# Sparse attention and two MLPs: how and when the weights are converted, and the order of the instructions

## The chip, the cores and the metric

The kernel runs on one core of one Trainium2 chip. The metric is the device time in microseconds (us); the kernel before took 1215.54 us, the median of three runs (1215.2 to 1216.38). TensorE is called PE here, VectorE DVE, ScalarE ACT, GpSimd POOL; SP is the engine whose queue issues all of the kernel's DMAs.

## The reference

```python
# q, k, v: 4 batches, 8 heads, 576 positions, head width 64, float32
scores = q @ k.T / sqrt(64)
keep only scores >= (row maximum - tau), softmax over the kept ones
x = (attn @ v) with heads side by side          # 2304 tokens x 512
h = x @ w_in                                    # 512 -> 2048
g = max(h, 0) + alpha * min(h, 0)
x = g @ w_out                                   # 2048 -> 512
h = x @ w2_in
g = where(h > 0, h, exp(min(h, 0)) - 1)
out = g @ w2_out
```

The weights of both MLPs arrive as 64-bit floats, 32 MiB in all.

## The kernel before

**Attention.** A unit is a batch and a pair of heads; 16 units of 9 jobs each make 144 jobs, a job being 128 query rows (or the 64 left over of both heads). A table of due times (`AT`, line 353) gives each stage of a job its place, and everything of the attention stage is issued through the `Pinned` wrappers (line 78), which keep the written order on each engine. In the trace such instructions carry line 84.

**The weights.** PE multiplies in fp32r, so each weight is kept as a high and a low part. A piece is the input half (`part` 0) or the output half (`part` 1) of block f of one layer, 128 partitions x 512; there are 2 layers x 16 blocks x 2 = 64 pieces. `conversion` (line 115) takes a piece from the 64-bit words: two ACT operations (lines 126, 127), two DVE operations (129, 130), a DVE and a POOL operation (133, 135), ACT writes the high part (137), DVE the low part (139) and the load of the piece three places on is issued. It is a generator of five steps, and one piece is worked on at a time.

The first 8 blocks of layer 0 (`FIRST`, 16 pieces) are converted beside the attention jobs, one step for every 1.5 jobs (`beside`, line 501). The last 8 blocks are converted in the first chunk of layer 0, where `convert_to` (line 154) runs two pieces to their end ahead of each block's first use. The 32 pieces of layer 1 are converted in the last chunk of layer 0, as blocks come free, and in the first chunk of layer 1. There the engines are the plain ones (not pinned), and a scheduler orders the instructions by priority; the activation's instructions (`tc.high_priority`, line 418) go ahead.

**The MLPs.** Tokens go in chunks of 512: four whole chunks and one of 256 for each layer. For each of 16 blocks f, `hidden` (line 408) runs 12 matmuls into one PSUM bank (line 415), and DVE, ACT and POOL make from it the activation's high and low part (lines 421 to 432); two blocks later (`LAG`) `outer` (line 441) runs 12 matmuls (452 or 455) into four accumulators. After the last block `evacuate` (line 435) moves accumulators 0 and 2 by ACT and 1 and 3 by DVE into `o`, which has two buffers, and a DMA stores each one; the third evacuation so waits for the first one's store. `load_in` (line 390) fetches the next chunk's input in four parts and splits each into high (ACT, 404) and low (DVE, 405). For the very first chunk it runs beside the last attention jobs, through the pinned engines (lines 499 to 505).

**The start.** `load_unit` (line 176) loads each head's k and q in the order k, q, q's tail for each half; `tau` is loaded after the first unit and its values (line 488), and the scale `sc` (line 491) made from it is needed by the first evacuations of q.

Of the kernel before, what the change touches and what calls it, by code (L numbers as in the profile page):

```python
# [20 lines left out]
def sparse_attention_two_mlps(  # L21
# [29 lines left out]
    FIRST = 8  # L51
# [6 lines left out]
    inp = ctx.enter_context(tc.tile_pool(name="inp", bufs=1))  # L58
# [8 lines left out]
    sc = const.tile([P, 1], F32, name="sc")  # L67
    alpha = const.tile([P, KFF], F32, name="alpha")
    x_d = [dram.tile([P, KDM, S], F32, name=f"x{b}") for b in range(B)]
    y_d = [dram.tile([P, KDM, M], F32, name=f"y{c}") for c in range(NCH)]  # L70
# [15 lines left out]
    plain = nc.vector, nc.scalar, nc.gpsimd  # L86
    pe, dve, act, pool = (Pinned(engine) for engine in (nc.tensor, nc.vector, nc.scalar, nc.gpsimd))
    pinned = dve, act, pool
# [26 lines left out]
    def conversion(dve, act, pool):  # L115
        i = converted[0]
        converted[0] += 1
        layer, f, part = pieces[i]
        if part == 0:
            wt[layer, f] = wps[f >= FIRST].tile([P, 2, 2, DM], F32R, tag="w", name="w")  # L120
        hi, lo = wt[layer, f][:, part, 0, :], wt[layer, f][:, part, 1, :]
# [7 lines left out]
        dve.tensor_scalar(out=x, in0=x, scalar1=TOP, scalar2=BOTTOM, op0=ALU.min, op1=ALU.max)  # L129
        dve.tensor_scalar(out=bits, in0=bits, scalar1=5, scalar2=2,  # L130
                                op0=ALU.logical_shift_left, op1=ALU.logical_shift_right)
        yield
        dve.scalar_tensor_tensor(out=bits, in0=upper, scalar=0xC0000000, in1=bits,  # L133
                                       op0=ALU.bitwise_and, op1=ALU.bitwise_or)
        pool.tensor_tensor(out=bits, in0=bits, in1=t, op=ALU.add)  # L135
        yield
        act.activation(out=hi, in_=x, func=AF.Copy)  # L137
        yield
# [3 lines left out]
    started = [None]  # L142


    def convert_step(limit, engines=plain):
        if started[0] is None:
            if converted[0] >= limit:
                return False
            started[0] = conversion(*engines)
        if next(started[0], "end") == "end":  # L150
            started[0] = None
        return True

    def convert_to(layer, f):
        n = 2 * (layer * KFF + f) + 2
        while convert_step(n) and (converted[0] < n or started[0] is not None):
            pass

    def w_in(layer, f, kk, part):
        return wt[layer, f][:, 0, part, kk * P:(kk + 1) * P]  # L160

    def w_out(layer, f, part):
        return wt[layer, f][:, 1, part, :]
# [12 lines left out]
    def load_unit(u):  # L176
# [3 lines left out]
        raws[u] = []  # L180
        for h in range(2):
            kr = raw.tile([KB, HS // KB, P], F32, tag="kr", name="kr", bufs=4)
            qr = raw.tile([P, NKT + 1, P], F32, tag="qr", name="qr", bufs=4)
            for a, cols in halves():
                rows = k[b, 2 * hp + h, a * HS:(a + 1) * HS, :]
                nc.sync.dma_start(out=kr[:, :, cols], in_=rows.rearrange("(t p) d -> p t d", p=KB))
                rows = q[b, 2 * hp + h]
                nc.sync.dma_start(out=qr[:, 0:NKT, cols], in_=rows[0:MAIN, :].rearrange("(t p) d -> p t d", p=P))
                nc.sync.dma_start(out=qr[0:TAIL, NKT, cols], in_=rows[MAIN:S, :])
            raws[u].append((kr, qr))  # L190
# [15 lines left out]
    def prep(u, i):  # L206
# [4 lines left out]
        if i < 2:  # L211
            kr = raws[u][i][0]
            for t in range(HS // KB):
                pe.transpose(ps[:, t * KB:(t + 1) * KB], kr[:, t, :], ident[0:KB, 0:KB])
        if i == 0:
            for h in range(2):
                pe.transpose(ps[:, HS + h * TAIL:HS + (h + 1) * TAIL], raws[u][h][1][0:TAIL, NKT, :],
                             ident[0:TAIL, 0:TAIL])
        if i >= 2:
            qr = raws[u][i - 2][1]  # L220
            for t in range(NKT):
                pe.transpose(ps[:, t * P:(t + 1) * P], qr[:, t, :], ident)
        return ps

    def keep_prep(u, i, ps):
        kt, qt = turned_in[u]
        if i < 2:
            act.activation(out=kt[:, i, :], in_=ps[:, 0:HS], func=AF.Copy)
# [3 lines left out]
        if i >= 2:  # L232
            act.activation(out=qt[:, i - 2, 0:MAIN], in_=ps, func=AF.Copy, scale=sc)
# [123 lines left out]
    def attention(beside):  # L357
# [24 lines left out]
        for i in range(2 * len(jobs) // 3):  # L382
            put(1.5 * i + AT["beside"], beside, 1.5 * i)
# [6 lines left out]
    def load_in(layer, j, dve=nc.vector, act=nc.scalar):  # L390
        n = min(M, NT - j * M)
        hi, lo = (inp.tile([P, KDM, M], F32R, tag="in", name="in", bufs=4) for _ in range(2))
        for kk in range(KDM):
            r = inp.tile([P, M], F32, tag="r", name="r", bufs=3)
            at = 0
            while layer == 0 and at < n:
# [148 lines left out]
```

## Time and profile before

| what | value |
|---|---|
| median of three runs | 1215.54 us |
| the profiled execution, its own time | 1218.32 us |
| its span | 1216.5 us |
| PE busy | 1150.3 us (95%) |
| DVE busy | 625.7 us (51%) |
| ACT busy | 517.7 us (43%) |
| POOL busy | 460.0 us (38%) |
| mean granted TensorE clock | 0.986 |

The span runs from the first to the last instruction; the time has some 1.8 us around it. A share of busy time is a mean over stages with different limits, so the page is read together with the views that cut the span into stages.

### The profile page before, as it was taken

How to read it: one execution, taken by the hardware profiler on the slowest of the kernel's cores; microseconds unless marked ns; L12 is line 12 of the kernel's file. 1: busy time of each engine (PE TensorE's matmuls, PEld its weight loads, DVE VectorE, ACT ScalarE, POOL GpSimd, SP SyncE). 2: the span in 40 equal slices, each digit the busy share in tenths (PEclk: the TensorE clock that was granted, in tenths of full speed). 3: DMA queues.
4: the chain of work that ended last, by engine and by line, in shares of the span. 5: the costliest groups of instructions: out<-in, count | busy, mean ns of one | idle time of the engine just before them, and what ended most of it. 6: DMA issues, size and time to landing. Idle time of an engine off the chain costs nothing.

```text
span 1216.5 us, 16463 instructions
## 1 busy us (share of the span) xinstructions
PE 1150.3 (95%) x5936; PEld 864.6 (71%) x5936; DVE 625.7 (51%) x1151; ACT 517.7 (43%) x988; POOL 460.0 (38%) x598
## 2 busy tenths in 40 slices
PE   6999999999899889999999999779899999999998
PEld 3555555555457678888888889667788888888887
DVE  3777877877856973223223236899732232131222
ACT  3877877877864432112111114565432232232222
POOL 1655656654553442222222224645422222222222
PEclk9999999998999999999999999989999999999999
DMA  6434334343312322001001004453110010010000
GB/s 154 115 103 123 97 88 106 97 103 104 99 47 79 122 87 70 1 1 57 1 1 65 1 2 137 137 161 121 32 70 1 1 57 1 1 40 1 1 35 18
DMA packets 116880, 77.10 MB, mean 63 GB/s; under 512 B 83264, under 2 KB 103744, under 8 KB 116800
## 3 DMA queue, kind: packets, MB, share of 16 engines
q1 hardware_dynamic: 116800, 76.06, 21.6%
q8 instruction: 47, 0.77, 0.3%
q14 instruction: 33, 0.27, 0.1%
HBM read 61.87 MB, written 14.16 MB: 62 GB/s over the span
## 4 chain that ended last, share of the span: by engine, by line
PE 54%; DVE 10%; POOL 3%; ACT 2%; issue 1%; DMA 0%; POOLq 0%; DVEq 0%; ACTq 0%
PE psh L415 26%; PE psa L455 15%; PE psa L452 13%; DVE x L133 3%; POOL x L135 2%; DVE w L139 2%; DVE x L130 2%; DVE x L129 1%; DVE g L427 1%; ACT w L137 1%; DVE g L421 1%; PE pst L84 1%; DVE g L425 0%; POOL gl L432 0%; ACT t L127 0%
## 5 line engine op out<-in xcount | busy, mean ns | idle before, releaser
L415 PE MATMUL psh<-in,w 128*128 128x512 f32 (+1 forms) x1920 | 421.2, 370 | 0.0
L432 POOL TENSOR_TENSOR gl<-g,gh 128x512 fp32r<-128x512 f32 (+1 forms) x160 | 193.2, 1208 | 546.3 <-ACT gh L431 499.8
L415 PEld LDWEIGHTS psh<-in,w 128*128 128x128 f32 x1920 | 338.3, 189 | 63.5
L431 ACT ACTIVATE gh<-g 128x512 fp32r<-128x512 f32 (+1 forms) x160 | 93.9, 587 | 297.1 <-DVE g L427 297.0
L452 PE MATMUL psa<-gh,w 128*128 128x512 f32 (+1 forms) x640 | 151.9, 381 | 18.1 <-ACT gh L431 18.0
L455 PE MATMUL psa<-w,gh 128*128 128x512 f32 x576 | 151.4, 403 | 9.3 <-ACT gh L431 9.3
L421 DVE TENSOR_SCALAR g<-psh,alpha 128x512 f32<-128x512 f32 (+1 forms) x80 | 55.6, 696 | 200.8 <-PE psh L415 186.1
L425 DVE TENSOR_SCALAR g<-g 128x512 f32<-128x512 f32 (+1 forms) x80 | 45.6, 570 | 208.8 <-ACT g L424 208.1
L452 PEld LDWEIGHTS psa<-gh,w 128*128 128x128 f32 x640 | 113.8, 192 | 44.4 <-ACT gh L431 21.8
L84 DVE TENSOR_REDUCE st<-ps 128x1 f32<-128x576 f32 x144 | 108.8, 755 | 68.9 <-PE ps L84 68.1
L455 PEld LDWEIGHTS psa<-w,gh 128*128 128x128 f32 x576 | 108.9, 192 | 36.4 <-ACT gh L431 11.4
L84 PEld LDWEIGHTS pst<-ident,e 128*128 128x128 f32 (+1 forms) x720 | 76.8, 139 | 70.4 <-POOL st L84 20.6
L84 PE MATMUL pst<-ident,e 128*128 128x128 f32 (+1 forms) x720 | 116.3, 289 | 7.0 <-ACT pt L84 4.2
L84 PE MATMUL ps<-kt,qt 64*128 64x288 f32 (+1 forms) x640 | 115.2, 469 | 5.6 <-DVE e L84 5.4
L84 DVE SCALAR_TENSOR_TENSOR e<-ps,st,e 128x576 f32<-128x576 f32 x144 | 116.0, 806 | 5.8 <-ACT e L84 4.5
L84 ACT ACTIVATE pt<-pst 128x512 f32<-128x512 f32 (+2 forms) x240 | 109.9, 463 | 13.2 <-PE pst L84 11.2
L84 POOL TENSOR_SCALAR e<-e,st 128x576 f32<-128x576 f32 x144 | 112.3, 780 | 8.0
L84 ACT ACTIVATE e<-ps,st 128x576 f32<-128x576 f32 x144 | 106.6, 740 | 4.7 <-DVE st L84 4.7
L427 DVE SCALAR_TENSOR_TENSOR g<-psh,g 128x512 f32<-128x512 f32 (+1 forms) x160 | 101.7, 636 | 4.3
L424 ACT ACTIVATE g<-psh 128x512 f32<-128x512 f32 (+1 forms) x80 | 44.1, 553 | 137.2 <-PE psh L415 136.6
L84 PE MATMUL pst<-pt,vt 128*64 128x256 f32 (+3 forms) x576 | 91.0, 417 | 0.0
L135 POOL TENSOR_TENSOR x<-x,t 128x512 uint32<-128x512 uint32 x48 | 69.5, 1450 | 42.5 <-DVE x L133 37.4
(47 smaller groups left out, 994.2 us busy)
## 6 DMA issues: line engine op xcount, KB each, us to landing
r<-in_moe_w_in_dram SPq DMA_DIRECT2D x32, 512.0 KB, 3.8
r<-in_moe_w_out_dram SPq DMA_DIRECT2D x32, 512.0 KB, 3.5
qr<-in_q_dram SPq DMA_DIRECT2D x64, 128.0 KB, 2.4
kr<-in_k_dram SPq DMA_DIRECT2D x64, 72.0 KB, 2.3
x<-xt SPq DMA_DIRECT2D x16, 288.0 KB, 2.5
out_dram<-o SPq DMA_DIRECT2D x18, 256.0 KB, 2.0
vt<-in_v_dram SPq DMA_DIRECT2D x32, 128.0 KB, 2.4
y<-o SPq DMA_DIRECT2D x16, 256.0 KB, 2.1
```

What stands on the lines that cost most here:

```text
L84: return lambda *args, **named: tc.keep_in_program_order(made(*args, **named))
L133: dve.scalar_tensor_tensor(out=bits, in0=upper, scalar=0xC0000000, in1=bits, op0=ALU.bitwise_and, op1=ALU.bitwise_or)
L135: pool.tensor_tensor(out=bits, in0=bits, in1=t, op=ALU.add)
L415: nc.tensor.matmul(out=ps[:, 0:n], lhsT=w_in(layer, f, kk, wpart), rhs=parts[xpart][:, kk, 0:n], start=(i == 0), stop=(i == 3 * KDM - 1))
L421: nc.vector.tensor_scalar(out=g[:, 0:n], in0=ps[:, 0:n], scalar1=0.0, scalar2=alpha[:, f:f + 1], op0=ALU.min, op1=ALU.mult)
L424: nc.scalar.activation(out=g[:, 0:n], in_=ps[:, 0:n], func=AF.Exp)
L425: nc.vector.tensor_scalar(out=g[:, 0:n], in0=g[:, 0:n], scalar1=1.0, scalar2=-1.0, op0=ALU.min, op1=ALU.add)
L427: nc.vector.scalar_tensor_tensor(out=g[:, 0:n], in0=ps[:, 0:n], scalar=0.0, in1=g[:, 0:n], op0=ALU.max, op1=ALU.add)
L431: nc.scalar.activation(out=hi[:, 0:n], in_=g[:, 0:n], func=AF.Copy)
L432: nc.gpsimd.tensor_tensor(out=lo[:, 0:n], in0=g[:, 0:n], in1=hi.bitcast(F32)[:, 0:n], op=ALU.subtract)
L452: nc.tensor.matmul(out=a[m][:, 0:n], lhsT=w_out(0, f, wpart)[:, m * P:(m + 1) * P], rhs=g[:, 0:n], start=start, stop=stop)
L455: nc.tensor.matmul(out=a[m], lhsT=g[:, m * P:(m + 1) * P], rhs=w_out(1, f, wpart), start=start, stop=stop)
```

## The change

- `FIRST` becomes 10: 20 pieces are converted beside the attention jobs, one step for every 1.25 jobs.
- In the MLP stages pieces are converted in rounds: `convert_round` starts a piece and advances each piece in flight by one step, with up to four in flight. One round follows each block of the first chunk, and three of every four blocks of the next three chunks.
- Layer 1's pieces are converted in those three chunks of layer 0. Their parts are stored to DRAM (`w_d`, two stores of 256 KB for each piece) and fetched back in the last chunk of layer 0 by `reload`, one DMA of 1 MB for each block, issued when layer 0 has used the block for the last time.
- Outside the attention stage the two `tensor_scalar` operations of a conversion become `scalar_tensor_tensor` with a broadcast column as second input; all subtractions that make a low part on DVE become `scalar_tensor_tensor` (times 1, minus).
- All instructions of the MLP stages go through the pinned engines, so each engine runs them in the order of the text; `tc.high_priority` goes.
- `load_in` fetches a chunk with one DMA (two where it crosses batches) and splits it over six calls from block 6 on. For the first chunk, the DMA and one high part stand beside the attention jobs; the rest follows them.
- `tau` is loaded first; `load_unit` brings k, both tails and q of head 0 before head 1, and `prep` follows that order.

```diff
-    FIRST = 8
+    FIRST = 10
+    w_d = [dram.tile([P, 2, 2, DM], F32, name=f"w{f}") for f in range(KFF)]
...
-        x = stage.tile([P, DM], F32, tag="x", name="x")
-        t = stage.tile([P, DM], U32, tag="t", name="t")
+        x = stage.tile([P, DM], F32, tag="x", name="x", bufs=4)
+        t = stage.tile([P, DM], U32, tag="t", name="t", bufs=3)
         act.activation(out=x, in_=upper.bitcast(F32), func=AF.Abs)
         act.activation(out=t, in_=lower, func=AF.Copy, scale=2.0 ** -29)
         yield
+        if layer == 0 and f < FIRST:
+            dve.tensor_scalar(out=x, in0=x, ...)
+            dve.tensor_scalar(out=bits, in0=bits, ...)
+        else:
+            dve.scalar_tensor_tensor(out=x, in0=x, scalar=TOP, in1=bottom.to_broadcast([P, DM]), ...)
+            dve.scalar_tensor_tensor(out=bits, in0=bits, scalar=5, in1=two.to_broadcast([P, DM]), ...)
+        if layer == 0 and f < FIRST:
+            yield
         dve.scalar_tensor_tensor(out=bits, in0=upper, scalar=0xC0000000, in1=bits, ...)
         pool.tensor_tensor(out=bits, in0=bits, in1=t, op=ALU.add)
+        load_piece(i + 3)
         yield
+        if layer == 1:
+            hi, lo = t.bitcast(F32R), x.bitcast(F32R)
         act.activation(out=hi, in_=x, func=AF.Copy)
+        if layer == 1:
+            nc.sync.dma_start(out=w_d[f][:, part, 0, :], in_=t.bitcast(F32))
         yield
-        dve.tensor_tensor(out=lo, in0=x, in1=hi.bitcast(F32), op=ALU.subtract)
-        load_piece(i + 3)
+        dve.scalar_tensor_tensor(out=lo, in0=x, scalar=1.0, in1=hi.bitcast(F32), op0=ALU.mult, op1=ALU.subtract)
+        if layer == 0:
+            converted_parts.append(f)
+        else:
+            nc.sync.dma_start(out=w_d[f][:, part, 1, :], in_=x)
...
+    def reload(f):
+        wt[f] = new_block(f)
+        nc.sync.dma_start(out=wt[f].bitcast(F32), in_=w_d[f])
+    def convert_round(limit):
+        if converted[0] < limit:
+            active.append(conversion(converted[0]))
+            converted[0] += 1
+        active[:] = [piece for piece in active if next(piece, "end") != "end"]
...
-            nc.tensor.matmul(out=ps[:, 0:n], ...)
-        with tc.high_priority(offset=100):
+            pe.matmul(out=ps[:, 0:n], ...)
...
     def chunk(n):
         layer, j = steps[n]
+        coming = load_in(*steps[n + 1]) if n + 1 < len(steps) else iter(())
         for f in range(KFF + LAG):
             if f < KFF:
-                convert_to(layer, f)
+                if n == 0:
+                    convert_to(f)
                 hidden(layer, j, f)
-            if f == KFF // 2 and n + 1 < len(steps):
-                list(load_in(*steps[n + 1]))
+            if f >= 6:
+                next(coming, None)
             if f >= LAG:
                 outer(layer, j, f - LAG)
                 if layer == 0 and j == NCH - 1:
-                    convert_to(1, f - LAG)
+                    reload(f - LAG)
+            if layer == 0 and f < KFF and (j == 0 or f % 4 < 3):
+                convert_round(2 * KFF * (1 if j == 0 else 2))
...
+    nc.sync.dma_start(out=tau_sb, in_=tau.rearrange("(o n) -> o n", o=1).to_broadcast([P, 1]))
     load_unit(0)
     load_values(0)
-    nc.sync.dma_start(out=tau_sb, in_=tau.rearrange("(o n) -> o n", o=1).to_broadcast([P, 1]))
...
-    def beside(j):
-        if j > 6:
-            convert_step(2 * FIRST, pinned)
-        if j > 100 and j % 6 == 0:
+    def beside(i):
+        if i > 4:
+            convert_step(2 * FIRST)
+        if i == 80 or i == 95:
             next(first_in, None)
```

## Rows read from the trace of the kernel before

**Rows 1.** Busy time by stretch: stretch, length; PE, PEld, DVE, ACT, POOL; clock, DMA share, GB/s.
```profile
369.44:443.00 73.56, 64.98 (x264) 51.20 (x263) 66.91 (x87) 33.98 (x59) 34.59 (x26) 0.95 0.35 113
443.00:735.00 292.00, 292.00 (x1266) 237.34 (x1265) 88.42 (x128) 46.67 (x78) 70.31 (x54) 1.00 0.08 26
735.00:902.00 167.00, 146.31 (x771) 124.45 (x770) 129.60 (x199) 82.54 (x151) 81.09 (x62) 0.95 0.34 108
```

**Rows 2.** Chain that ended last: start us, us, what; x36 are three hidden blocks together.
```profile
469.48 8.19 PE psh L415 x36
...
558.17 8.19 PE psh L415 x36
...
735.56 2.89 PE psh L415 x24
...
902.20 8.17 PE psh L415 x36
...
990.52 8.17 PE psh L415 x36
```

**Rows 3.** Timeline of PE: start us, us, engine line, names, [idle before <- releaser].
```profile
369.44 6.57 PE L415 MATMUL psh<-in,w 128*128 128x512 f32 x27
...
412.57 2.12 PE L452 MATMUL psa<-gh,w 128*128 128x512 f32 x8 [2.39 <-ACT gh L431]
...
743.98 1.60 PE L415 MATMUL psh<-in,w 128*128 128x256 f32 x12
...
746.84 1.60 PE L415 MATMUL psh<-in,w 128*128 128x256 f32 x12
```

**Rows 4.** Timeline of DVE in the first chunk, one block's turn.
```profile
400.48 0.74 DVE L421 TENSOR_SCALAR g<-psh,alpha 128x512 f32<-128x512 f32 x1
...
402.47 0.68 DVE L427 SCALAR_TENSOR_TENSOR g<-psh,g 128x512 f32<-128x512 f32 x1
403.07 0.67 DVE L139 TENSOR_TENSOR w<-x,w 128x512 fp32r<-128x512 f32 x1
...
404.11 0.43 DVE L130 TENSOR_SCALAR x<-x 128x512 uint32<-128x512 uint32 x1
404.57 1.69 DVE L133 SCALAR_TENSOR_TENSOR x<-r,x 128x512 uint32<-128x512 uint32 x1
...
408.67 0.75 DVE L421 TENSOR_SCALAR g<-psh,alpha 128x512 f32<-128x512 f32 x1
```

**Rows 5.** Timeline of POOL in the same stretch.
```profile
404.42 1.29 POOL L432 TENSOR_TENSOR gl<-g,gh 128x512 fp32r<-128x512 f32 x1 [2.42 <-ACT gh L431]
```

**Rows 6.** Waits of the whole span: total us, times, longest us.
```profile
ACT o L437 <- DMA y<-o: 8.9, 4, 2.3
```

**Rows 7.** Busy time by stretch, the busiest moments of the DMA engines.
```profile
24.00:26.00 2.00, 2.00 (x10) 1.24 (x9) 2.00 (x6) 0.74 (x1) 1.07 (x3) 1.00 1.02 376
...
806.00:816.00 10.00, 6.49 (x28) 4.72 (x26) 8.18 (x15) 5.94 (x12) 4.87 (x3) 1.00 0.66 222
```

**Rows 8.** Timeline of SP: the stores of units 10, 11 and 12, counted from 0.
```profile
267.57 0.54 SPq L349 DMA_DIRECT2D x<-xt  x1
...
288.96 0.54 SPq L349 DMA_DIRECT2D x<-xt  x1
...
319.06 0.34 SPq L349 DMA_DIRECT2D x<-xt  x1
```

**Rows 9.** Timeline between the last two of these stores, DVE.
```profile
290.29 0.69 DVE L84 TENSOR_TENSOR in<-r,in 128x512 fp32r<-128x512 f32 x1 [3.93 <-ACT in L84]
```

**Rows 10.** Busy time by stretch, steady attention.
```profile
100.00:200.00 100.00, 94.33 (x647) 54.66 (x645) 76.97 (x176) 80.47 (x167) 60.03 (x115) 1.00 0.38 97
```

**Rows 11.** Timeline of the start.
```profile
9.14 0.34 PE L84 MATMUL pst<-ident,qr 64*128 64x64 f32 x1 [3.17 <-DMA qr<-in_q_dram]
...
12.55 0.15 DVE L491 TENSOR_SCALAR sc<-tau_sb 128x1 f32<-128x1 f32 x1 [10.86 <-DMA tau_sb<-in_tau_dram]
...
15.05 2.29 PE L84 MATMUL ps<-kt,qt 64*128 64x288 f32 x8
```

More of the change, by code (lines that the diff above doesn't have):

```diff
@@ L154, in convert_to @@
[L154 to L163, printed above, removed]
+        if layer == 0 and f < FIRST:
+            dve.tensor_scalar(out=x, in0=x, scalar1=TOP, scalar2=BOTTOM, op0=ALU.min, op1=ALU.max)
+            dve.tensor_scalar(out=bits, in0=bits, scalar1=5, scalar2=2,
+                              op0=ALU.logical_shift_left, op1=ALU.logical_shift_right)
+        else:
+            dve.scalar_tensor_tensor(out=x, in0=x, scalar=TOP, in1=bottom.to_broadcast([P, DM]), op0=ALU.min,
+                                     op1=ALU.max)
+            dve.scalar_tensor_tensor(out=bits, in0=bits, scalar=5, in1=two.to_broadcast([P, DM]),
+                                     op0=ALU.logical_shift_left, op1=ALU.logical_shift_right)
@@ new lines, in reload, with convert_step @@
+    def reload(f):
+        wt[f] = new_block(f)
+        nc.sync.dma_start(out=wt[f].bitcast(F32), in_=w_d[f])
+    active, converted_parts = [], []
+    def convert_step(limit):
+        if not active and converted[0] < limit:
+            active.append(conversion(converted[0]))
+            converted[0] += 1
+        if active and next(active[0], "end") == "end":
+            active.pop()
+    def convert_round(limit):
+        if converted[0] < limit:
+            active.append(conversion(converted[0]))
+            converted[0] += 1
+        active[:] = [piece for piece in active if next(piece, "end") != "end"]
+        return bool(active)
@@ L169, in sparse_attention_two_mlps, with convert_to, w_in, w_out @@
+    def convert_to(f):
+        while converted_parts.count(f) < 2:
+            convert_round(2 * KFF)
+    def w_in(f, kk, part):
+        return wt[f][:, 0, part, kk * P:(kk + 1) * P]
+    def w_out(f, part):
+        return wt[f][:, 1, part, :]
     units = [(b, hp) for b in range(B) for hp in range(NP)]
@@ L381, in attention @@
                 put(j + AT["keep_prep"], lambda u, i, held=held: keep_prep(u, i, *held), job.u + 1, job.i)
-        for i in range(2 * len(jobs) // 3):
-            put(1.5 * i + AT["beside"], beside, 1.5 * i)
+        for i in range(len(jobs) * 4 // 5):
+            put(1.25 * i + AT["beside"], beside, i)
         for _, _, what, args in sorted(todo, key=lambda t: t[:2]):
@@ L435, in evacuate @@
+        hi = mlp.tile([P, M], F32R, tag="gh", name="gh", bufs=LAG + 1)
+        lo = mlp.tile([P, M], F32R, tag="gl", name="gl", bufs=LAG + 1)
+        act.activation(out=hi[:, 0:n], in_=g[:, 0:n], func=AF.Copy)
+        pool.tensor_tensor(out=lo[:, 0:n], in0=g[:, 0:n], in1=hi.bitcast(F32)[:, 0:n], op=ALU.subtract)
+        gs[layer, j, f] = hi, lo
     def evacuate(m, to, src):
         if m % 2 == 0:
-            nc.scalar.activation(out=to, in_=src, func=AF.Copy)
+            act.activation(out=to, in_=src, func=AF.Copy)
```

151 lines of the change are left out of this document (72 added, 79 removed).

## The prediction

> **What bounds the kernel now.** I read the busy time by stretch first, to see which engine is full in which stage. From 443 to 735 us PE is busy in all of 292.0 us, and DVE in 88 [rows 1]: there PE alone is the bound and nothing done to another engine can help. In the two stretches with conversions PE is busy 65.0 of 73.6 and 146.3 of 167.0 us while DVE reaches 66.9 and 129.6 [rows 1]. The chain of waits gives the price. Three hidden blocks in a row mark a chunk's start: a full chunk of layer 0 takes 558.17 - 469.48 = 88.7 us (5.54 for each block), one of layer 1 takes 990.52 - 902.20 = 88.3 us [rows 2]. The first chunk runs from 369.44 [rows 3] to 469.48, 100.0 us. The half chunk of layer 0 and layer 1's first chunk run from 735.56 to 902.20, 166.6 us, where PE needs 16 x 2.86 (746.84 - 743.98, one block of 256 tokens [rows 3]) = 45.8 and 88.3, so 134.1. Some 11.3 and 32.5 us are lost in these two places.
>
> The timeline says by whom. PE waits 2.39 us for the activation's high part [rows 3], which waits for DVE, and DVE's turn of one block, from one L421 to the next, takes 8.19 us without a gap: two pieces and one activation [rows 4]. POOL adds to it: L133 starts at 404.57, while POOL's `gl` runs from 404.42 to 405.71 [rows 5], and takes 1.69 us, where L139 alone takes 0.67 [rows 4]. So DVE operations with two inputs in SBUF stand still while POOL works.
>
> In the attention stage PE is busy 94% [rows 10]; the stores of units 11 and 12 lie 30.1 us apart where a usual distance is 21.4 [rows 8]. In between DVE waits 3.93 us for the high part of the first chunk's input [rows 9], with the jobs' own DVE work queued behind: 30.1 - 21.4 = 8.7 us.
>
> **The change, part by part.** The sum is made against the profiled execution, 1218.3 us, which lies 2.8 us above the median of 1215.5.
>
> *First chunk.* 20 pieces are then ready, 12 are left, at one round for each block. The last pieces finish in rounds 13 and 14 (counted from 0), before blocks 15's two halves are used, so `convert_to` never runs a piece ahead of PE. DVE's turn becomes 0.74 + 0.68 for the activation and four operations of about 0.68 (L139 and L427 unblocked [rows 4]), 4.14 us. POOL's two operations hold DVE for 1.69 - 0.68 = 1.0 us each when they meet it. The sum of a piece comes as DVE goes over to the next activation, which reads PSUM; so I count one, 5.15 us, under PE's 5.54. With both it is 6.15, and twelve turns fall 7.3 us behind; `outer` follows the end of its `hidden` by four groups of 2.77 us, 11.1, of which the activation's chain needs 0.74 + 0.68 + about 0.6 + 1.29 = 3.3. Even then it just holds. What comes new: three high parts and the low parts of the first input now stand after the attention's last instruction, and block 0 waits for them, two operations of 0.67 [rows 4], 1.3 us. And 9 of the first 36 matmuls, which now run among the attention's last instructions (27 are left at 369.44 [rows 3]), come back to this chunk; 88.7 us holds them all. I take 88.7 + 1.3 + 1.5 for small waits = 91.5, so -8.5 us (bounds -11.3 and -0.5, the latter with 8 us of lag in the open).
>
> *Swap to two-input operations.* In this trace an L130 takes 0.43 us unblocked, a two-input operation 0.68 [rows 4]: 0.25 us more, twice a piece, 44 pieces, 22 us of DVE time, hidden by PE as above. No row shows an input of one broadcast column. It costs between nothing of POOL's hold (as L427 with one SBUF input) and the full 1.0 us for each meeting (as L133); I take the latter, because it too is read from SBUF. The Trainium skill (SBUF — State Buffer, Who interferes with whom) says that a DVE instruction with two SBUF inputs, as one in a two-port mode, locks out a GpSimd instruction that reads SBUF and is locked out by it. By that rule the swap buys nothing against POOL and only lengthens two operations, which speaks against it; L133's 1.69 us agrees.
>
> *Layer 1's pieces* go through 36 rounds in chunks 1 to 3 (35 are needed), where DVE is now idle 70% [rows 1]. Three turns of at most 6.15 and one of 1.42 for each four blocks are 19.9 us against PE's 22.2. Loads and stores come to 1 MB in 5.54 us, 190 GB/s, where 222 have been moved over 10 us and 376 over 2 us [rows 7]. I count nothing; without that cover each turn above 5.54 would be paid 35 times.
>
> *The boundary.* Conversions go, 32.5 us with them. What is late next is the DMA queue. `reload` asks for 1.05 MB every 2.86 us, 367 GB/s, and the busiest row moved 376 [rows 7]. The first reload goes out after three `hidden` and one `outer`, 5.7 us into the half chunk; by its end at 45.8, some 38 us after the first bytes, 15 blocks and the next input, 16.8 MB, are asked for and 14.3 moved at 376 GB/s. The rest, 2.5 MB or 6.6 us, lies ahead of the first store of the half chunk's results. Now the third and fourth evacuation wait up to 2.3 us for such a store [rows 6]; then it is some 9. ACT and DVE hold their order, so layer 1's first activation stands behind these evacuations: 9.2 + 0.6 + 0.55 + 0.43 + 0.68 + 0.6 (estimates by operations of the same size), 12.0 us after the half chunk's end, where PE has three hidden blocks, 8.3 us, to do. A wait of 3.8 us. With less than 376 it is longer; at 344, 8 us. I take 5: 134.1 + 5 = 139.1, so -27.5 us (bounds -32.5, no wait, and -17, the wait at 300 GB/s being 15). Weights themselves are not late: the last is needed 45.8 + 15 x 5.52 = 128.6 us in, and 17.8 MB have until then. The chunk's input, behind four reloads, lands some 24 us in, in front of block 8's high part on ACT, which `outer` needs at 27.2.
>
> *Attention.* The low parts of the first input no longer stand among the jobs: -8.7 us (bounds -8.7 and -6, a high part being left). Four more pieces are 20 more steps. Steady attention leaves PE idle 5.7 us in 100 [rows 10], that is 4.7 units of 6 steps, 0.2 us a step if the steps cause all of it: +4 us. Bounds are 0 and 4 x (0.67 + 0.68 + 2 x 0.43) = 8.8 us, all of their DVE time exposed [rows 4].
>
> *Start.* The first scores stand at 15.05, behind `sc`, which had `tau` at 12.55; the queries were there at 9.14 [rows 11]. With `tau` first they come an issue, 0.54 us [rows 8], later, and the scores could start some 3 to 4 us earlier, but the next unit's loads keep their place. I take -2 (0 to -4). The two memsets and the other places of `prep` hide behind these loads.
>
> Sum: -8.5 - 27.5 - 8.7 + 4 - 2 = -42.7; 1218.3 - 42.7 = 1175.6 for the profiled execution, 1173 for the median.
>
> **The rivals.** *A, no new wait:* the boundary costs nothing, the first chunk 90.0, the four pieces nothing and the start gives 4: -10 - 32.5 - 8.7 - 4 = -55, 1160 us. For it: all engines but PE have room. Against it: the stores stand behind 2.5 MB.
> *B, the reload stream holds the activation:* at 300 GB/s 5.4 MB lie ahead, the wait is 15 us and the time 1183. For it: only 2 us moved 376 GB/s. Against it: that stretch moved small rows, a reload has 8 KB in each partition.
> *C, slower, DVE and POOL lock each other out:* each of a round's four operations meets a POOL operation, so a turn takes 1.42 + 4 x 1.69 = 8.2 us, today's length with two pieces [rows 4]. Twelve turns of the first chunk lose 32 us, and each four blocks in chunks 1 to 3 take 3 x 8.2 + 1.4 = 26.0 instead of 22.2, twelve times, 46 us: 1173 + 78 = 1251. It decides from a turn of about 7.2 us on, where 20 and 23 us make up for the gain. Against it: there are two POOL operations in a round, and one of them meets PSUM work. The Trainium skill's rule above is this mechanism, an exclusive lock and not a sharing.
> *D, attention pays:* a step at another place in the jobs' order holds up DVE or ACT as the input's low part did, 0.75 us for each of 20 steps: 15 instead of 4, 1184 us. For it: 3.93 us behind one such wait [rows 9]. Against it: 80 steps now pass without one.
>
> **How the numbers follow.** The forecast gets 0.58, A 0.12, B 0.14, D 0.10, C 0.06. A measurement of this kernel can tell about 0.2%, 2.4 us, from no change. C gives slower, 0.06; its lower edge and the worst of B and D together give the same, 0.02; the rest, 0.92, faster. The range reaches from just under A, 1158, past B and D and some of their sum, 1197, and leaves C out: with its 0.06 and the tails of the others some 0.15 stay outside. All cases but C are of one sign.
>
> **What would show it.** In the profile after, a chunk's start should follow the first one by some 91 us and DVE's turns in the first chunk be near 5.2 with PE full; the half chunk and layer 1's first should take about 139 us, with a wait of ACT or DVE `o` for the store `y` of 8 to 10 us as the one large wait; the units of attention should be even, at 21.5 us, with no wait of DVE for `in`; the first scores should start near 12 us. The prediction is wrong if PE stands idle in chunks 1 to 3, if a round makes DVE fall behind block by block, or if the units grow beyond 22.5 us.

## The result, and the profile after

The changed kernel takes 1180.38 us (median of 4 runs, 1177.41 to 1180.89) beside 1215.37 us for the kernel before on the same chip (4 runs, 1213.33 to 1216.38): a ratio of 0.971, 95% interval 0.9689 to 0.973. 1173 was predicted. The profiled execution took 1180.63 us, 1178.8 of them span, beside 1218.32 and 1216.5 before; the sum of the prediction had 1175.6 for it.

Busy time by stretch of the kernel after: stretch, length; PE, PEld, DVE, ACT, POOL; clock, DMA share, GB/s. The stretches are the attention, the first chunk, chunks 1 to 3, the half chunk with layer 1's first chunk, and the rest.

```profile
0.00:367.13 367.13, 328.80 (x2192) 188.99 (x2193) 265.01 (x599) 273.26 (x557) 201.46 (x394) 1.00 0.39 100
367.13:457.32 90.19, 89.60 (x387) 72.42 (x386) 70.35 (x88) 34.44 (x61) 39.10 (x28) 1.00 0.32 97
457.32:723.20 265.88, 265.88 (x1154) 216.51 (x1154) 193.97 (x243) 91.78 (x162) 112.00 (x80) 1.00 0.42 143
723.20:862.00 138.80, 136.35 (x769) 118.53 (x769) 40.78 (x77) 32.20 (x60) 32.39 (x32) 0.99 0.41 148
862.00:1178.80 316.80, 312.36 (x1441) 256.73 (x1439) 81.66 (x149) 81.38 (x148) 73.75 (x64) 1.00 0.06 21
```

Its chain of waits, the chunks' starts (all pinned instructions stand on L87 now, the line of the helper):

```profile
457.32 8.18 PE psh L87 x36
...
545.95 8.18 PE psh L87 x36
...
862.00 8.21 PE psh L87 x36
...
950.98 8.21 PE psh L87 x36
...
961.98 2.77 PE psh L87 x12
```

The ledger, from the same places before [rows 2, 3]; the last column is the prediction's:

| stretch | before | after | difference | predicted |
|---|---|---|---|---|
| to the first hidden block | 369.4 | 367.1 | -2.3 | -6.7 |
| first chunk | 100.0 | 90.2 | -9.8 | -8.5 |
| chunks 1 to 3 | 266.1 | 265.9 | -0.2 | 0 |
| half chunk and layer 1's first | 166.6 | 138.8 | -27.8 | -27.5 |
| the rest | 314.3 | 316.8 | +2.5 | 0 |

So the gain stands where it was forecast, in the two stages where DVE held PE up [rows 1]. The attention kept 4.4 us of what it was to give, and the later chunks of layer 1 became slower, 950.98 - 862.00 = 88.98 us instead of 88.3 [rows 2].

A part of the gain may be TensorE's clock. Before, it stood at 0.95 of full speed in the mean in both of these stages [rows 1]; since its lower level, 1.2 GHz, is half of the upper, that is 0.05 x 2 x 73.56 and 0.05 x 2 x 167.0, some 7 and 17 us at 1.2 GHz. After, it is 1.00 and 0.99. PE's work in those 24 us took up to 12 us longer than at 2.4 GHz; with the waits for DVE these stretches went too, and how much of the 37.6 us was theirs is not told apart.

One block's turn in the first chunk, DVE and then POOL; [idle before <- releaser]. It answers to [rows 4, 5]:

```profile
399.14 0.75 DVE L87 TENSOR_SCALAR g<-psh,alpha 128x512 f32<-128x512 f32 x1 [0.43 <-PE psh L87]
399.93 0.69 DVE L87 SCALAR_TENSOR_TENSOR g<-psh,g 128x512 f32<-128x512 f32 x1
400.54 0.68 DVE L87 SCALAR_TENSOR_TENSOR w<-x,w 128x512 fp32r<-128x512 f32 x1
401.13 0.69 DVE L87 SCALAR_TENSOR_TENSOR x<-x,bottom 128x512 f32<-128x512 f32 x1
401.85 1.67 DVE L87 SCALAR_TENSOR_TENSOR x<-x,two 128x512 uint32<-128x512 uint32 x1
403.56 0.69 DVE L87 SCALAR_TENSOR_TENSOR x<-r,x 128x512 uint32<-128x512 uint32 x1
404.68 0.75 DVE L87 TENSOR_SCALAR g<-psh,alpha 128x512 f32<-128x512 f32 x1 [0.43 <-PE psh L87]
```

```profile
401.48 1.50 POOL L87 TENSOR_TENSOR gl<-g,gh 128x512 fp32r<-128x512 f32 x1 [1.39 <-issue]
404.33 1.30 POOL L87 TENSOR_TENSOR x<-x,t 128x512 uint32<-128x512 uint32 x1 [1.35 <-DVE x L87]
```

A turn is 0.75 + 0.69 + 0.68 + 0.69 + 1.67 + 0.69 = 5.17 us of work, 5.54 from one to the next, and the rest is DVE waiting for PE: PE is the bound. POOL's `gl` holds one operation, the one with the broadcast column `two`, until 403.52, 0.54 after its own end at 402.98. The other POOL operation falls on the activation, which reads PSUM and is not held.

The boundary, SP, ACT, DVE and PE; it answers to [rows 6]:

```profile
729.81 38.56 SPq L166 DMA_DIRECT2D w<-w  x15
769.52 0.80 SPq L501 DMA_DIRECT2D y<-o  x2
```

```profile
776.68 0.38 ACT L87 ACTIVATE o<-psa 128x256 f32<-128x256 f32 x1 [7.19 <-DMA y<-o]
```

```profile
777.05 0.42 DVE L87 COPY o<-psa 128x256 f32<-128x256 f32 x1 [7.40 <-DMA y<-o]
```

```profile
779.45 3.12 PE L87 MATMUL psa<-w,gh 128*128 128x512 f32 x8 [1.87 <-ACT gh L87]
```

Fifteen reloads go out ahead of the half chunk's last two stores. The third and fourth evacuation wait 7.2 and 7.4 us for these stores, where the longest such wait was 2.3; PE runs dry for 1.87 us, and right behind that the clock stood at 1.2 GHz for 3.4 us (from 780.3).

### The profile page after: what moved, and what is told of

Read it like the earlier page. It is cut to its first block, busy times and chain, and to the rows that moved or that the text cites. A ratio compares the mean times of both kernels' runs of the same rounds, so it can differ in the third digit from the quotient of the medians.

```text
span 1178.8 us, 16654 instructions
## 1 busy us (share of the span) xinstructions
PE 1133.0 (96%) x5936; PEld 853.2 (72%) x5936; DVE 651.8 (55%) x1153; ACT 513.1 (44%) x988; POOL 458.7 (39%) x598
## 4 chain that ended last, share of the span: by engine, by line
PE 67%; DMA 1%; ACT 0%; DVE 0%; issue 0%; SPq 0%; DVEq 0%; ACTq 0%
PE psa L87 34%; PE psh L87 32%; DMA y<-o 1%; PE pst L87 1%; DVE g L87 0%; DMA out_dram<-o 0%; ACT o L87 0%; ACT gh L87 0%; DVE o L87 0%; ACT xt L87 0%; DVE il L87 0%; ACT pt L87 0%; ACT g L87 0%; DMA x<-xt 0%; SPq L505 0%
## 5 line engine op out<-in xcount | busy, mean ns | idle before, releaser
L87 POOL TENSOR_TENSOR gl<-g,gh 128x512 fp32r<-128x512 f32 (+1 forms) x160 | 200.3, 1252 | 490.4 <-ACT gh L87 418.7
L87 PE MATMUL psh<-ih,w 128*128 128x512 f32 (+1 forms) x1280 | 385.9, 369 | 0.4 <-ACT ih L87 0.4
L87 PEld LDWEIGHTS psh<-ih,w 128*128 128x128 f32 x1280 | 233.7, 188 | 45.0 <-ACT ih L87 0.8
L87 ACT ACTIVATE gh<-g 128x512 fp32r<-128x512 f32 (+1 forms) x160 | 94.5, 591 | 330.8 <-DVE g L87 319.2
L87 PE MATMUL psh<-il,w 128*128 128x512 f32 (+1 forms) x640 | 236.8, 370 | 0.2 <-DVE il L87 0.2
L87 DVE TENSOR_SCALAR g<-g 128x512 f32<-128x512 f32 (+1 forms) x80 | 38.2, 477 | 253.9 <-ACT g L87 253.8
L87 PE MATMUL psa<-w,gh 128*128 128x512 f32 x576 | 148.7, 398 | 2.2 <-ACT gh L87 2.2
L87 DVE TENSOR_REDUCE st<-ps 128x1 f32<-128x576 f32 x144 | 108.6, 754 | 75.6 <-PE ps L87 75.1
L87 PE MATMUL psa<-gh,w 128*128 128x512 f32 (+1 forms) x640 | 147.8, 373 | 0.6 <-ACT gh L87 0.6
L87 PEld LDWEIGHTS psh<-il,w 128*128 128x128 f32 x640 | 120.2, 188 | 22.1 <-DVE il L87 0.5
L87 PEld LDWEIGHTS pst<-ident,e 128*128 128x128 f32 (+1 forms) x720 | 74.5, 137 | 80.0 <-issue 22.6
L87 PE MATMUL pst<-ident,e 128*128 128x128 f32 (+1 forms) x720 | 114.8, 285 | 17.1 <-POOL e L87 9.8
L87 PEld LDWEIGHTS psa<-gh,w 128*128 128x128 f32 x640 | 112.5, 188 | 23.5 <-ACT gh L87 0.8
L87 PEld LDWEIGHTS psa<-w,gh 128*128 128x128 f32 x576 | 107.6, 189 | 27.7 <-ACT gh L87 2.8
L87 DVE SCALAR_TENSOR_TENSOR e<-ps,st,e 128x576 f32<-128x576 f32 x144 | 115.9, 805 | 4.9 <-ACT e L87 4.0
L87 ACT ACTIVATE pt<-pst 128x512 f32<-128x512 f32 (+2 forms) x240 | 109.7, 464 | 15.8 <-PE pst L87 13.4
L87 ACT ACTIVATE g<-psh 128x512 f32<-128x512 f32 (+1 forms) x80 | 44.3, 553 | 165.3 <-PE psh L87 163.6
L87 POOL TENSOR_SCALAR e<-e,st 128x576 f32<-128x576 f32 x144 | 111.1, 772 | 9.7 <-DVE st L87 1.8
L87 PE MATMUL ps<-kt,qt 64*128 64x288 f32 (+1 forms) x640 | 111.4, 455 | 0.3 <-DVE e L87 0.3
L87 POOL TENSOR_TENSOR x<-x,t 128x512 uint32<-128x512 uint32 x64 | 82.3, 1287 | 72.3 <-DVE x L87 69.9
L87 ACT ACTIVATE e<-ps,st 128x576 f32<-128x576 f32 x144 | 106.6, 740 | 2.3 <-DVE st L87 2.3
L87 DVE SCALAR_TENSOR_TENSOR g<-psh,g 128x512 f32<-128x512 f32 (+1 forms) x160 | 102.1, 638 | 5.5
```

What stands on the lines that cost most here:

```text
L87: return lambda *args, **named: tc.keep_in_program_order(made(*args, **named))
```

## The experiments

Two theories stood against each other for each place. In the attention, that the forecast's terms were right but each mis-sized, against a step that stands badly in the jobs' order (D). For the first chunk, that the rounds brought the gain, against the two blocks moved away from it. For the boundary, that the stores wait behind the reloads, against conversions or the reload stream itself. Times without an interval are one run each, and there the spans of the profile are compared.

### What a piece costs the attention

Only one block, or eight blocks, converted in the attention; the other blocks of the first ten take block 0's weights. Eight blocks at the old pace and at the new one:

```diff
-            convert_step(2 * FIRST)
+            convert_step(2)        # 16 for eight blocks
...
-            put(1.25 * i + AT["beside"], beside, i)
+            put(1.5 * i + AT["beside"], beside, i)      # the old pace alone
...
```

> The kernel after with two pieces converted beside attention instead of 20; blocks 1 to 9 of layer 0 take block 0's weights, so 18 conversions are left out and the result is another. It shows what a unit of attention takes without conversion steps. If the steps are what makes units of 22.15 us on average (units 1 to 12 of the kernel after), units without them take the 20.9 of unit 13, which has hardly any: 12 x 1.2 = 15 us less, some 1165. If the units are slower for another reason (the new order of loads and of the preparation of q and k), they stay near 22 and the time above 1175.

> The kernel after with 16 pieces beside attention, one step for every 1.5 jobs as before; blocks 8 and 9 take block 0's weights, so four conversions are left out. Both theories expect the units of before, 21.3 us, so some 12 x 0.85 = 10 us less than the kernel after, 1170. If units stay near 22.1, neither the number nor the places of the steps is the cause, and the order of loads is.

> The kernel after with 16 pieces at its own pace of one step for every 1.25 jobs; blocks 8 and 9 take block 0's weights, so four conversions are left out. The steps end about 25 jobs earlier. Theories place and number: units with steps stay at 22.1, some three units lose their steps and fall to 20.9, 3 to 4 us less, 1176. A theory by which the last pieces alone cost (each piece 3 us): 12 us less, 1168.

Measured, in this order: 1157.66, 1173.67 and 1172.86 us; the last store of the attention at 347.2, 360.7 and 362.5, beside 368.0 with all 20 pieces. With one block the stores lie 20.22 us apart, unit after unit (20.9 had been expected); at the new pace the units are those of the changed kernel as long as steps go on (22.4, 22.8, 21.1 ...), and fall to 20.2 to 20.8 once they end. The busy time of a steady stretch says what a step does, of the kernel after and then of the one with one block; it answers to [rows 10]:

```profile
100.00:200.00 100.00, 91.55 (x620) 52.54 (x618) 76.38 (x173) 78.38 (x162) 58.63 (x112) 1.00 0.42 110
```

```profile
100.00:200.00 100.00, 98.84 (x682) 57.28 (x679) 68.44 (x160) 75.45 (x155) 50.05 (x115) 1.00 0.34 86
```

Without steps PE is busy 98.8%, with them 91.6%, and no other engine is above 78.4%: steps cost by the waits that they put among the jobs, not by filling an engine. The price of one step: six a unit in the kernel before and with eight blocks at the old pace, whose units are some 21.3 us, (21.3 - 20.22) / 6 = 0.18; at the new pace 7.2 a unit, whose mean is 22.15, (22.15 - 20.22) / 7.2 = 0.27. One unit of that mean, of 24.07 us, also holds the one high part of the first input that was left among the jobs (ACT `ih` at 304.49, and right behind it PE waits 1.87); without that unit the mean is 21.97 and the price 0.24.

### Whether it is the place of the steps

A job's time has fixed places for its operations. At 1.25 the steps fall on four different ones; here they fall on two:

```diff
-            put(1.25 * i + AT["beside"], beside, i)
+            put(round(2.5 * i) / 2 + AT["beside"], beside, i)
```

> The kernel after with all 20 pieces, each step moved by at most a quarter of a job, so that steps stand 0.2 or 0.7 behind a job's number as before, and never 0.45 or 0.95. Theory place (a step at the new places stands ahead of a job's operation that is due and holds it up): units fall back to 21.3 to 21.6, 7 to 10 us less, 1170 to 1173. Theory number (what counts is how many steps a unit has, 7.2 instead of 6): units stay at 22.1 and the time within 2 us of 1180.

Measured: 1178.75 us, ratio 0.9698 (0.968 to 0.9716), units of 22.25, 22.66, 22.81 and 20.97 us where the changed kernel has 22.45, 22.36, 22.76 and 21.13, last store 367.0. At these places the steps cost the same; what changed the units in the other runs is how many of them a unit has.

### The input's split, and the start, each alone

The kernel before with the low part of the first input one call behind its high part, so that DVE need not wait for it:

```diff
             act.activation(out=hi[:, kk, 0:n], in_=r[:, 0:n], func=AF.Copy)
+            yield
             dve.tensor_tensor(
```

> The kernel before with one edit: in loading the first chunk's input, the low part is made one step after the high part. If the long wait of DVE for the high part cost what the distance of two stores showed, the distance falls from 30.1 to some 21.4 and the time by 8.7 us, 1206.5. If the units were slow there for the work itself, nothing changes (within 2 us).

Measured: 1215.11 us; span 1213.3 instead of 1216.5, last store 367.6 instead of 370.3. The long distance of [rows 8] is gone, but with it 30.1, 20.8 and 18.1 us have become 22.9, 25.0 and 19.0, 2.2 us less in all; the other 0.5 is there at the first store already. So the wait that was read in [rows 9] accounts for 2.7 us of the 8.7 at most. The clock is in this too. The stretch of 30.1 us in the kernel before:

```profile
288.96:319.06 30.10, 24.41 (x139) 14.15 (x137) 22.52 (x47) 21.66 (x44) 15.21 (x27) 0.83 0.31 90
```

A mean clock of 0.83 is 10.2 us at 1.2 GHz (6.8 from 291.5 on, 3.4 from 312.0 on); with the low part later the clock is low there for 3.4 us alone, from 325.2 on. Unit against unit, 3.4 us at 1.2 GHz cost up to 1.5 us (last section), so the clock accounts for up to 4.5 of the 8.7.

The kernel before with the new order of the first loads alone (`tau` first, the queries' tails together, `prep` in the order q and k arrive):

```diff
+    nc.sync.dma_start(out=tau_sb, in_=tau.rearrange("(o n) -> o n", o=1).to_broadcast([P, 1]))
     load_unit(0)
...
-    nc.sync.dma_start(out=tau_sb, in_=tau.rearrange("(o n) -> o n", o=1).to_broadcast([P, 1]))
...
```

> The kernel before with the start of the kernel after: tau first, keys, tails and queries of head 0 before head 1, and the preparation in that order. The prediction gave this 2 us. The trace after shows unit 1 starting 6.0 us earlier (27.4 against 33.4). If the loads do it, 6 us less, 1209.5; if a part of the 6 us is due to the later start of the steps, 2 to 4 us less.

Measured: 1212.64 us, span 1210.8 (-5.7), last store 364.5 (-5.8). The first reduction of scores starts at 12.8 instead of 16.4, and unit 1 at 27.7 instead of 33.4: the second unit's loads gain more than the first's. Also in the kernel after:

```profile
12.61 0.76 DVE L87 TENSOR_REDUCE st<-ps 128x1 f32<-128x576 f32 x1 [8.69 <-PE ps L87]
```

### The first chunk: rounds, or fewer pieces

The changed kernel with the old division, eight blocks ahead at the old pace and 16 pieces in the first chunk:

```diff
-    FIRST = 10
+    FIRST = 8
...
-            put(1.25 * i + AT["beside"], beside, i)
+            put(1.5 * i + AT["beside"], beside, i)
...
```

> The changed kernel with eight blocks in the attention, as the kernel before had, a step at every 1.5 jobs: 16 pieces are left to the first chunk, in rounds. It sets the two halves of the trade apart that the change makes with its two extra blocks. Theory: the last store of the attention at about 361 (as in the run with 16 pieces at the old pace), 19 rounds are needed ahead of the last block where 15 have gone by, four forced at about 4 us, the first chunk 104 to 106, in all about 1188: the rounds alone bring little and the two blocks moved into the attention are what makes the first chunk TensorE's. Rival: DVE's total of work in that chunk, about 88 of 90 us, fits; the first chunk takes at most 93, in all 1176.

Measured: 1181.72 us, ratio 0.9703 (0.9685 to 0.9722): the time of the changed kernel, between the 1188 of the theory and the 1176 of its rival. The last store moves to 357.3, and the first chunk, 356.4 to 458.2, takes 101.8 us, no less than the 100.0 before. The theory's mechanism is there, forced rounds at the last blocks, two of them with 2.6 us of wait for a weight and one with 1.35, at three quarters of its price (11.6 us over the changed kernel's 90.2, for 14 to 16). Behind each of the two longer waits the clock fell, which is the 0.97:

```profile
356.50:458.20 101.70, 94.29 (x387) 74.05 (x386) 85.39 (x104) 41.34 (x73) 45.50 (x32) 0.97 0.35 107
```

```profile
428.21 0.73 PE L87 MATMUL psh<-ih,w 128*128 128x512 f32 x2 [2.59 <-DVE w L87]
```

So the rounds by themselves gave the first chunk next to nothing: 2.0 of its 101.8 us are the nine matmuls that stood ahead of this stretch in the kernel before [rows 3]. The two blocks that were moved away gave the 9.8 us, and cost the attention as much. This kernel also settles the input's split, because up to unit 11 (counted from 0) its stores stand where those of the kernel with the new start alone do. The stores of `xt` on SP, first with the start alone, then with eight blocks, then of the changed kernel (x2 is the last two, the second at the end of the time given):

```profile
283.94 0.54 SPq L351 DMA_DIRECT2D x<-xt  x1
313.29 0.34 SPq L351 DMA_DIRECT2D x<-xt  x1
334.06 0.54 SPq L351 DMA_DIRECT2D x<-xt  x1
352.17 12.69 SPq L351 DMA_DIRECT2D x<-xt  x2
```

```profile
283.96 0.54 SPq L382 DMA_DIRECT2D x<-xt  x1
306.13 0.34 SPq L382 DMA_DIRECT2D x<-xt  x1
326.54 0.54 SPq L382 DMA_DIRECT2D x<-xt  x1
344.65 12.99 SPq L382 DMA_DIRECT2D x<-xt  x2
```

```profile
292.26 0.54 SPq L382 DMA_DIRECT2D x<-xt  x1
316.33 0.54 SPq L382 DMA_DIRECT2D x<-xt  x1
337.27 0.54 SPq L382 DMA_DIRECT2D x<-xt  x1
355.38 13.00 SPq L382 DMA_DIRECT2D x<-xt  x2
```

The split out of the jobs is worth 364.86 - 357.64 = 7.2 us. In the first of the three, 6.8 us at 1.2 GHz, from 302.9 on, are part of that, worth up to 3 us; they begin in a wait of PE of 3.28 us, and whether they belong to the split is open. The two more blocks with the quicker pace cost 368.38 - 357.64 = 10.7. The kernel with eight blocks has 3.4 us at 1.2 GHz in its attention (from 105), which made one unit 1.5 us longer, and the changed kernel has none, so like for like it is 12.2.

### The swap to two-input operations

The changed kernel with the operations of one input everywhere:

```diff
-        if layer == 0 and f < FIRST:
...
-        else:
-            dve.scalar_tensor_tensor(out=x, in0=x, scalar=TOP, in1=bottom.to_broadcast([P, DM]), op0=ALU.min,
...
+        dve.tensor_scalar(out=x, in0=x, scalar1=TOP, scalar2=BOTTOM, op0=ALU.min, op1=ALU.max)
...
```

> The kernel after with the two operations with a broadcast column made tensor_scalar again in all pieces. Theory hidden (DVE has room under PE in chunks 0 to 3): within 2 us of the kernel after, and DVE busy some 20 us less. Theory lock (the two-port form holds POOL off and so the activation): first chunk over 92 us and the time 3 us or more above. A gain of over 2 us would say that DVE was on the path after all.

Measured: 1179.21 us, ratio 0.9702 (0.9681 to 0.9723); the first chunk 90.0 us:

```profile
366.80:456.80 90.00, 89.42 (x387) 72.25 (x386) 65.10 (x88) 34.38 (x61) 37.08 (x28) 1.00 0.30 97
```

DVE is busy 65.1 instead of 70.35 us, 5.25 / 24 = 0.22 us for each swapped operation, and the stage does not notice. The operations of one input are held by POOL as well: both of a piece together, 0.41 + 0.43 us when free (0.43 [rows 4]), take

```profile
400.76 1.93 DVE L87 TENSOR_SCALAR x<-x 128x512 f32<-128x512 f32 x2
```

beside `gl` here. The swap costs nothing and brings nothing.

### The boundary: the stores behind the reloads

The last six reloads behind the half chunk's stores:

```diff
-                if layer == 0 and j == NCH - 1:
+                if layer == 0 and j == NCH - 1 and f - LAG < 10:
                     reload(f - LAG)
+                if n == NCH and f == LAG:
+                    for b in range(10, KFF):
+                        reload(b)
```

> The kernel after with the reloads of blocks 10 to 15 issued after the stores of layer 0's last results instead of before them. The theory that these stores stand behind the reload stream: the waits of 7.2 and 7.4 us for the store fall to about 2.3, PE's wait of 1.87 us at layer 1's first block goes, with the slower matmuls behind it: 2 to 4 us less, 1177. Rival, the wait is the store's own time at that place: unchanged. If late weights take its place, PE waits at block 10 and the time is above 1180.

Measured: 1177.75 us, ratio 0.9688 (0.9669 to 0.9707); in the profile the boundary, 723.0 to 858.2, takes 135.2 us, 3.6 less than in the changed kernel. PE no longer waits behind the evacuations, and there is no stretch at 1.2 GHz. The evacuation that waited 7.19:

```profile
771.46 0.39 ACT L87 ACTIVATE o<-psa 128x256 f32<-128x256 f32 x1 [2.00 <-DMA y<-o]
```

The changed kernel without layer 1's conversions and reloads (layer 1 takes layer 0's weights):

```diff
...
-                    reload(f - LAG)
+                    pass
...
-                convert_round(2 * KFF * (1 if j == 0 else 2))
+                convert_round(2 * KFF)
```

> The changed kernel without layer 1's conversions, stores and reloads: layer 1 takes layer 0's weights, so 32 conversions and 16 reloads are left out. It measures what they cost where they now stand. Chunks 1 to 3 of layer 0 265.9 as with them (the conversions are hidden whole), the boundary about 134 instead of 138.8 (no reload ahead of the y stores). For layer 1's four later chunks, which took 88.98 us each instead of 88.32 before: theory A (the weights' being reloaded at the boundary, or the conversions, leaves something behind that slows them) 88.3, in all about 1173; theory B (the instructions' order or the place of the tiles does it, whatever fills them) 89.0 again, in all about 1176.

Measured: 1177.27 us, ratio 0.9674 (0.9658 to 0.9691). Chunks 1 to 3, the boundary, the rest:

```profile
458.30:724.10 265.80, 265.80 (x1153) 216.47 (x1152) 79.13 (x115) 39.27 (x67) 61.90 (x48) 1.00 0.07 22
724.10:859.40 135.30, 134.70 (x770) 117.60 (x769) 40.45 (x77) 32.46 (x61) 32.51 (x32) 1.00 0.08 28
859.40:1176.40 317.00, 312.51 (x1441) 256.86 (x1439) 81.85 (x149) 81.49 (x149) 73.83 (x64) 1.00 0.06 21
```

Without any of that work the boundary takes 135.3 us, as with all of it and late reloads. So 32 conversions, their loads, their 64 stores and, issued late, the reloads are hidden whole, and the 3.5 us between were the place of the `y` stores in the queue, with the short stretch at 1.2 GHz behind the wait. The rest of layer 1 takes 317.0 us here too: theory A falls, what slows it is not the reloaded weights, their values or the transfers.

### Nine blocks, and rounds in the attention's tail

Late reloads, nine blocks, a step at every 1.4 jobs; then the same with two rounds of the first chunk's pieces in the last jobs, where no step is left:

```diff
-    FIRST = 10
+    FIRST = 9
...
-        if i > 4:
+        if i in (96, 99):              # the second kernel alone
+            convert_round(2 * KFF)
+        elif 4 < i < 96:
             convert_step(2 * FIRST)
```

> The changed kernel with nine blocks (18 pieces) in the attention instead of ten, a step at every 1.4 jobs instead of 1.25, and blocks 10 to 15 reloaded behind layer 0's last stores, as in the run of the late reloads alone (1177.8 us). Theory (the first chunk has room for one round a block and no more: DVE's turn with a round is about 5.2 of the 5.54 us of a block): 14 pieces need 17 rounds ahead of the last block where 15 blocks have gone by, so two rounds are forced, about 4 us of DVE each; the first chunk goes from 90.2 to about 97, the attention's last store from 368.0 to 365 or 366, in all about 1181. Rival (what a forced round needs was saved up, since DVE is busy 70 of 90 us in that chunk): the first chunk stays within 91.5, in all 1175 to 1176, and nine blocks would be the better split.

> The run with nine blocks in the attention and late reloads (1178.2 us), with two rounds of the first chunk's pieces put into the attention's last jobs, where no step is left and VectorE waits 12.2 us for the last stores' input. If the first chunk is set by how many rounds VectorE must take ahead of the last block (17 needed, 15 blocks go by), these two are the two that were forced: the first chunk falls from 94.4 to 90 or 91 us without the 2.5 us wait of TensorE at the last blocks, the attention's last store stays at 365 to 366, and the whole comes to 1174 to 1175. Rival: the sum of attention and first chunk has been 457 to 459 whatever the number of blocks, because the rounds cost the attention what they save later; then the last store moves to 368 or more and the time stays at 1177 to 1178.

Measured: 1178.15 us, ratio 0.9685 (0.9669 to 0.9701), and 1176.05 us, ratio 0.9672 (0.9658 to 0.9685). With nine blocks the last store comes at 365.2 and the first chunk takes 94.4 us, with one wait of 2.53 us for a weight; both as the theory has it, a little smaller. The two rounds in the tail do bring the first chunk to PE's bound:

```profile
369.90:460.00 90.10, 89.52 (x387) 72.33 (x386) 74.03 (x93) 35.42 (x63) 40.38 (x29) 1.00 0.33 103
```

but in the profiled execution the attention gave it back: the distance between the 14th and the 15th store grew from 18.1 to 22.7 us and the last store came at 370.9. That execution was the slowest of the five (1179.8; the fastest 1174.54), and TensorE stood at 1.2 GHz in three short stretches of its attention (from 32.3, 305.4 and 353.2), so how much of the loss is the rounds' is not settled. By the comparisons with the kernel before, this division is the fastest that was tried: 0.9672 (0.9658 to 0.9685) beside 0.9709 (0.9689 to 0.973) for the change as made. No single one of its three steps (late reloads, nine blocks, rounds in the tail) is told apart from zero.

## Why the prediction was right, point by point

**The whole.** 1180.4 instead of 1173, faster as forecast; 35.0 us were gained by the medians and 42.7 forecast. By the profiled execution the sum missed by 1180.63 - 1175.6 = 5.0 us: the attention (+4.4) and layer 1's later chunks (+2.5), less 1.3 in the first chunk and some tenths elsewhere. That the attention's share is no more than 4.4 is in part luck: its three terms were off by -3.8, +1.5 and +6.7 and offset each other, and the profile before had 10.2 us at 1.2 GHz in its attention, the profile after none, which is worth up to 4.5.

**First chunk: the number right, its cause incomplete.** DVE's turn came out as chosen, with one of POOL's operations met: 5.17 for 5.15. The lag of 7.3 us that was feared did not arise, and the first block waits 0.35 and 0.23 us for the input's parts instead of 1.3. But the step that credited this stage with 8.5 us and charged the pieces elsewhere with 4 made a gain out of a transfer: with the old division in rounds the chunk takes 101.8, and in the attention the pieces cost 10.7.

**The swap.** Right at both ends: 0.22 us more for each operation (0.25 predicted), a broadcast column is held by POOL as a full second input is (1.67 against 0.69), and all of it lies under PE. The rule of the Trainium skill (SBUF — State Buffer, Who interferes with whom), that two SBUF inputs make a DVE instruction share GpSimd's port under an exclusive lock, agrees with the trace: the held operation ends 0.54 us after POOL's, and the activation's first operation, which reads PSUM, takes its 0.75 us beside POOL's other one. That the swap buys nothing, which was worked out beside it, holds too (90.0 us without it).

**C (slower)** is excluded by the same rows: it needed a turn of 7.2 us.

**Chunks 1 to 3.** PE is busy 265.88 of 265.88 us with DVE at 194; without the conversions it is 265.8. Nothing, as counted.

**The boundary: right in size and in place.** 138.8 instead of 139.1, with the wait for `y` at 7.2 and 7.4 us (8 to 10 forecast). The 5 us of wait were, as measured, 1.87 us of PE standing still, some 1.7 for the stretch at 1.2 GHz in its wake (half of 3.4), which no step had, and the slower matmuls of layer 1; that they come to 4.7 in all is closer than the step earned. Rival A needed PE's wait to vanish, which late reloads alone bring about; B needed a stream of 300 GB/s, and while the reloads ran it was 369:

```profile
740.00:760.00 20.00, 20.00 (x172) 20.00 (x171) 8.94 (x19) 5.03 (x11) 5.16 (x7) 1.00 0.98 369
```

**The attention: three terms mis-sized, in both directions.** *Start:* -5.8 instead of -2. The step that failed is "the next unit's loads keep their place": unit 1 started 5.7 us earlier, beyond the 4 us at the end of the range. *Input's split:* -7.2 instead of -8.7, near enough; but the reading behind it was wrong, since taking away DVE's wait alone returned 2.7 at most, and up to 4.5 of the 8.7 were the clock. The -7.2 holds what the whole split among the jobs cost and up to 3 us of clock. *Four more pieces:* +10.7 instead of +4 (12.2 like for like), past the upper bound of 8.8. The price of 0.2 for a step was right for the old pace, 0.18. What was left out is that the steps' pace rises from one in 1.5 to one in 1.25 jobs, and each step then costs 0.27: the twenty new ones 20 x 0.27 = 5.4 and the other 80 another 80 x 0.09 = 7.2, 12.6 together. The runs with eight blocks show both parts: at the new pace, four pieces fewer end the attention 368.0 - 362.5 = 5.5 us earlier; and the new pace alone ends it 362.5 - 357.3 = 5.2 us later than the old one, 6.7 with the 1.5 us of clock. The bound was worked out from the new steps' own time and so could not see it. D had the larger cost, by another mechanism (a bad place); the run with two places shows no sign of it.

**The rest: an effect that no step had.** Layer 1's chunks are 0.66 us longer each. In the chain a hidden block takes 2.77 us there and 2.73 in layer 0 of the same kernel. It is the same with eight, nine or ten blocks ahead, with late reloads, and without reloads or conversions; the kernel before with the new start or the split input has 88.3. What is left is what all kernels built on the change share, the written-out order of the instructions and the input's new tiles; which of them it is was not tried.

**Units.** 22.15 us in the mean, under the 22.5 named as the mark of a wrong prediction, above the 21.5 forecast. The forecast had them even; they run from 20.9 to 24.1, and four of thirteen are above 22.5.

## What to carry to other kernels

Work interleaved into a tuned loop has a price that depends on its pace: moving more of it in makes the work that is already there dearer, so measure the loop with none of it and at two paces before a gain elsewhere is booked. When a stage gets faster because work was moved out of it, add both stages up: here two blocks moved gave 9.8 us to one and took 10.7 from the other, and the real gains were the second layer's conversions under a stage where PE is full (27.8 us), the input's split out of the jobs (7.2, up to 3 of them clock) and the start (5.8). Compare the clock of two profiles before a distance in one of them is put down to a wait. A stream of large loads put into a queue ahead of small stores delays whatever waits for those stores; issue what is needed late behind them.

## What the runs showed of the hardware that was not expected

A wait of PE of 1.87 us was followed by 3.4 us at 1.2 GHz, while the same kernel with waits of 0.35 and 0.23 us in the first chunk stayed at 2.4 GHz. The length of the wait alone does not decide: behind the high part in the attention PE waits 1.87 us too, up to 306.11, and stayed at 2.4 GHz, while in the kernels with one-input operations, with late reloads and without layer 1's conversions the same wait (1.87, 1.87 and 1.88 us) was followed by 3.4 us at 1.2 GHz; and in the kernel before a wait of 2.67 us (up to 766.86) was not. The short stretches at 1.2 GHz inside the attention come and go between kernels whose units are otherwise equal: one makes its unit up to 1.5 us longer (21.5 and 23.0 us for the same unit in the two kernels with eight blocks at the old pace), which is as much as some of the effects looked for there.

Matmuls of 512 columns that follow each other without a wait start 227 ns apart in layer 1's hidden blocks before, and 231 ns apart in the mean after (2.77 us for 12). The slower ones are not spread evenly: behind an `outer` the first eight lie 224 to 236 ns apart and the rest 226 or 227, as in layer 1's blocks before, so that three blocks in a row take 8.21 us, little more than the 8.17 before [rows 2]. It is so in each of the later chunks, and in the kernel without layer 1's conversions and reloads too.
